# Attention with beacon keys and a two-layer block: where the second layer's last groups stand among the next chunk's first layer

## The chip, the cores and the metric

One core of a Trainium2 chip runs the kernel. The metric is device time in microseconds: 332.71 us, the median of three runs (331.96 to 333.87). A profiled execution took 332.48 us.

## The reference

Attention over 8 sequences (B) with 8 heads (H), 576 tokens (S) and head size 64 (D). Each head's keys and values are preceded by 16 beacon keys and values, which every token may see; the rest is causal. Its output is the input of a two-layer block over 4608 tokens.

```python
k_all = np.concatenate([beacon_k, k], axis=2)
v_all = np.concatenate([beacon_v, v], axis=2)
scores = scale * np.matmul(q, k_all.transpose(0, 1, 3, 2))
causal[:, Nb:] = np.triu(np.ones((S, S), dtype=bool), k=1)
scores = np.where(causal, -1000000000.0, scores)
scores = scores - scores.max(-1, keepdims=True)
a = np.exp(scores)
a /= a.sum(-1, keepdims=True) + 1e-09
attn = np.matmul(a, v_all)
...
x = attn.transpose(0, 2, 1, 3).reshape(B * S, H * D)      # 4608 x 512
h = x @ w_in                                              # 512 x 2048
g = np.maximum(0.01 * h, h)
out = g @ w_out                                           # 2048 x 512
```

## The kernel before

**Attention.** Two heads make a pair; a sequence has four pairs, so there are 32 (g = 0 to 31). The scores stand transposed, keys on the partitions, for five chunks of keys. From pair 8 on the scores of all pairs are one long row of columns (1664 a pair), cut into tiles of 512 columns for both heads; `block(m)` does three tiles: its matmuls (L314), its exps on ScalarE (L329 for the first tile, one head each; L333 for the other two, both heads at once), and then on POOL the causal triangles (L289). The first tile's two heads lie in two PSUM buffers of the pool `ps_one`, the other two tiles in the pool `ps_sc`. `value(g, half)` multiplies probabilities with values (L359: 12 matmuls in half 0, 18 in half 1), and VectorE divides by the sums (L388, L389). `x_turn(g)` lets SP transpose the result by DMA into `xT` (L417, L425), where the first layer reads it.

**The two layers** work on nine chunks of 512 tokens. The first layer has 16 up groups a chunk (`up`, `moe1`): four matmuls of 512 columns into an `acc` of `ps_one` (L442; eight shorter ones in chunk 4), then a PReLU on ScalarE into `gT` (L450). The second layer has down groups (`down`, `moe2`). Chunk 0 has 16 plain ones (L512). The other chunks have 14, eight matmuls of 256 columns each (L539): seven products of a Strassen scheme, two token tiles each, in the order 1, 6, 2, 7, 5, 4, 3. Sums of parts of `gT` that the products need are made on VectorE (L616, `token_sums`), four operations after the eighth and four after the sixteenth up group; `due` hands out one of them at each group, and the third down group of a chunk takes all that are left. Product 1 reads PReLUs, product 6 is the first to read sums.

**PSUM.** `ps_one` has four buffers of one bank each. A tile holds a buffer from its first write to its last read. The second layer's accumulators are "a" (products 1 and 2, down groups 0 to 5), "b" (product 6, groups 2 and 3), "c" (products 7 and 4, groups 6 to 11) and "d" (products 5 and 3, groups 8 to 13).

**The order** is written out by hand up to pair 7. From there a list of events (L792 to L814) places blocks, value halves, loads, transposes and `finish` on a time line counted in pairs, sorted by time; every engine keeps the order in which the program was written. Between events the loop (L817 to L829) lets `fill()` put up and down groups, as many as the share of the time line asks for. A window ends with each sequence; `KEPT = 3` groups are left over at its end, and `finish` sets `held` to 3, so that `fill()` gives these first. Otherwise `fill()` gives an up group if one is possible, and turns are changed where both kinds are possible. Up groups of chunk i need down groups of chunk i - 2 to be done, and down groups of chunk i need all its up groups. Before a value half (L826) at least four groups must stand behind the last block, but only where no down group is left.

So the order of TensorE is fixed when the program is built. Around the first layer of chunk 3 it is (u3.0 is the first up group of chunk 3, d2.8 the ninth down group of chunk 2, V16.1 the second value half of pair 16, B11 block 11):

```
d2.4 B10 d2.5 d2.6 d2.7 d2.8 d2.9 V16.0 d2.10 d2.11 B11 V16.1 d2.12 d2.13
u3.0 u3.1 u3.2 V17.0 u3.3 u3.4 B12 u3.5 u3.6 u3.7 u3.8 V17.1 u3.9 u3.10 V18.0 u3.11 B13
u3.12 u3.13 u3.14 u3.15 V18.1 d3.0 V19.0 d3.1 d3.2 B14 V19.1 d3.3 d3.4
```

After the last value half, of pair 31, the order is d6.3 to d6.13, u7.0 to u7.15, then down groups of chunk 7 and up groups of chunk 8 by turns, then chunk 8's down groups.

Of the kernel before, what the change touches and what calls it, by code (L numbers as in the profile page):

```python
# [15 lines left out]
def kernel(  # L16
# [21 lines left out]
    NF = DF // 128  # L38
# [361 lines left out]
    def x_transposes(g, copy):  # L400
        b, hp = divmod(g, NPAIR)
        x_nat, _ = xs.pop(g)
        ps = ps_one.tile([128, 1024], BF16, name="tp", tag="one")
        for t, (q0, rows) in enumerate(QT):
            nc.tensor.transpose(
                ps[:, q0 : q0 + rows],
                x_nat[0:rows, t].rearrange("p e d -> p (e d)"),
                ident[0:rows, 0:rows],
            )
        copy(out=xT[:, hp, x_at(b) : x_at(b) + S], in_=ps[:, 0:S])  # L410
# [93 lines left out]
    def ND(i):  # L504
        return NF if i == 0 else 2 * len(PRODUCTS)
# [89 lines left out]

    done1, done2, at2, ready, turn, first_down, held = [0], [0], [0, 0], [0], [0], [0], [0]

    def fill():
        i1, fc = divmod(done1[0], NF)
        i2, n2 = at2  # L600
        can1 = i1 < ready[0] and (i1 < 2 or i2 > i1 - 2)
        can2 = i2 < NCH and i2 < i1 and done1[0] >= first_down[0]
        if held[0] and can2:
            held[0] -= 1
            down()
        elif can1 and (turn[0] == 0 or not can2):
            up()
        elif can2:
            down()
        return can1 or can2  # L610
# [14 lines left out]
    def up():  # L625
        i1, n = divmod(done1[0], NF)
        assert i1 < ready[0]
        fc = n if i1 == 0 else n // 2 + n % 2 * HF
        moe1(i1, fc)
        add_due()  # L630
        done1[0] += 1
        turn[0] = 1
        if i1 and n % (2 * SLICE) == 2 * SLICE - 1:
            due.extend((i1, op) for op in token_sums(i1, n // 2 + 1 - SLICE, n // 2 + 1))

    def down():
        add_due()
        if at2[1] == 2:
            add_all(at2[0])
        moe2(*at2)  # L640
        done2[0] += 1
        at2[1] += 1
        if at2[1] == ND(at2[0]):
            at2[:] = at2[0] + 1, 0
        turn[0] = 0
# [19 lines left out]
            )  # L665

    NG = B * NPAIR
    KEPT = 3

    def has(g):  # L670
        return 0 <= g < NG
# [3 lines left out]
    def chunks_with(g):  # L675
        return (g + 1) // NPAIR * S // 512

    def finish(g, eng=0):
        if eng < 2 and g in xs:
            x_transposes(g, (dve, act)[eng])  # L680
        ready[0] = chunks_with(g)
        if g % NPAIR == NPAIR - 1:
            turn[0] = 1
            held[0] = KEPT

    def run(steps):
        for step in steps.split():
# [7 lines left out]
            elif op == "e":  # L695
                value_ahead(*a)
            elif op == "x":
                finish(*a)
            elif op == "l":
                load_qk(*a)  # L700
# [39 lines left out]
    with order:  # L740
# [43 lines left out]
            for parts in tiles:  # L784
                triangles(parts)

        def has_down():
            return at2[0] < done1[0] // NF

        since = 0  # L790
        events = []
        for g in range(FIRST, NG):  # L792
# [14 lines left out]
        for g in range(FIRST, NG):  # L807
            events.append((g + 3.5, 2, finish, (g, 2)))
            if g % NPAIR == NPAIR - 1:
                ends.append(g + 3.5)  # L810
# [6 lines left out]
        for at, _, what, args in events:  # L817
            while w + 2 < len(ends) and at > ends[w + 1]:
                w, d0 = w + 1, done1[0] + done2[0]
            todo = NF * ready[0] + sum(ND(i) for i in range(ready[0])) - KEPT - d0  # L820
            aim = d0 + todo * (at - ends[w]) / (ends[w + 1] - ends[w])
            while done1[0] + done2[0] < aim and fill():
                pass
            if what is block:
                since = done1[0] + done2[0]
            elif what is value and not has_down():  # L826
                while done1[0] + done2[0] < since + 4 and fill():
                    pass
            what(*args)  # L829
        while at2[0] < NCH:  # L830
            fill()
# [30 lines left out]
```

## Time and profile before

| what | value |
|---|---|
| median of 3 runs | 332.71 us |
| profiled execution, its time | 332.48 us |
| its span, first to last instruction | 330.8 us |
| up groups' matmuls (L442) | 134.0 us busy |
| down groups' matmuls (L539) | 111.0 us busy in four rows (47.2, 32.9, 15.5, 15.4) |
| value matmuls (L359) | 39.5 us busy |
| PReLU (L450) | 83.0 us busy, 620 ns each |
| exps of the blocks (L329, L333) | 28.9 and 51.7 us busy |
| granted TensorE clock | 0.999 |

PE is TensorE, PEld its weight loads, DVE VectorE, ACT ScalarE, POOL GpSimd, SP SyncE. In the table of waits, each line has the waiting engine and line, what released it, the total in us, how often, and the longest. A wait that stands at PEld and at PE is one wait seen twice: the weight load waits first, and the matmul behind it. In the timeline a line has start and length in us, the engine, the line, the operation, and in brackets the idle time before it and what ended it. A PE row's first matmul can start some 0.2 us after its weights began to load.

### The profile page before, as it was taken

To read this page: it belongs to the slowest core of one execution; us is meant where nothing else is said; L and a number is where in the kernel's file an instruction comes from. 1 tells how busy PE (TensorE), PEld (TensorE's weight loads), DVE (VectorE), ACT (ScalarE), POOL (GpSimd) and SP (SyncE) were. 2 spreads that over 40 slices of the span, in tenths; PEclk is the share of its full clock that TensorE was granted. 3 is DMA by queue.
4 is the path that set the end of the run, shared out by engine and by line. 5 is a ranking of instruction groups with operands and counts; after the bars stand their busy time and mean duration, and the time that the engine had idled before them with its cause. 6 is when DMAs were issued, how large, how long until landed. Compare 5 with 4: busy or idle time off the path is not lost.

```text
span 330.8 us, 8482 instructions
## 1 busy us (share of the span) xinstructions
PE 317.8 (96%) x3401; PEld 213.1 (64%) x3429; DVE 132.5 (40%) x280; ACT 199.8 (60%) x336; POOL 183.2 (55%) x354
## 2 busy tenths in 40 slices
PE   8999999999899999999999999998999999999996
PEld 5574555455586557844778888655875695466685
DVE  3572357126443145414621453334442642333343
ACT  4969861678665784578645865587458514644420
POOL 8895968979987884669546976686221000000000
PEclk9999999999999999999999999999999999999999
DMA  8999999999999999999989999999431113000113
GB/s 134 140 204 178 153 209 121 179 181 131 180 111 169 158 157 142 131 164 102 145 122 154 109 146 113 184 120 155 55 100 37 36 21 127 2 0 34 64 43 117
DMA packets 155929, 39.93 MB, mean 121 GB/s; under 512 B 143041, under 2 KB 153153, under 8 KB 155889
## 3 DMA queue, kind: packets, MB, share of 16 engines
q0 software_dynamic: 99824, 18.54, 83.1%
q1 hardware_dynamic: 55792, 20.77, 38.7%
q8 instruction: 27, 0.44, 0.6%
q14 instruction: 14, 0.11, 0.1%
q10 hardware_dynamic: 272, 0.07, 0.1%
HBM read 37.22 MB, written 9.44 MB: 141 GB/s over the span
## 4 chain that ended last, share of the span: by engine, by line
PE 76%; DMA 8%; ACT 5%; DVE 4%; POOL 4%; issue 2%; SPq 0%; ACTq 0%; POOLq 0%
PE acc L442 34%; PE acc L539 25%; PE av L359 7%; PE sc L314 5%; DMA w_out_sb<-in_moe_w_out_dram 4%; PE acc L512 4%; DMA v_aug<-in_v_dram 3%; DVE gsum L616 2%; ACT aT L333 2%; ACT aT L329 2%; ACT gT L450 1%; DVE x_nat L389 1%; POOL gsum L158 1%; DMA xT<-x_nat 1%; POOL v_aug L214 1%
## 5 line engine op out<-in xcount | busy, mean ns | idle before, releaser
L442 PE MATMUL acc<-xT,w_in_sb 128*128 128x512 bf16 (+1 forms) x615 | 134.0, 357 | 1.9 <-DMA xT<-x_nat 0.5
L450 ACT ACTIVATE gT<-acc 128x512 bf16<-128x512 f32 x144 | 83.0, 620 | 56.9 <-PE acc L442 55.4
L442 PEld LDWEIGHTS <-w_in_sb 128*128 128x128 bf16 x640 | 59.6, 98 | 53.6 <-issue 4.3
L289 POOL TENSOR_SCALAR_AFFINE_SELECT aT<-aT 128x256 bf16<-128x256 bf16 (+2 forms) x160 | 59.8, 403 | 60.9 <-ACT aT L329 38.7
L539 PEld LDWEIGHTS <-gT 128*128 128x128 bf16 x512 | 48.9, 98 | 11.2 <-ACT gT L450 2.3
L333 ACT ACTIVATE aT<-sc 128x1024 bf16<-128x1024 f32 (+3 forms) x64 | 51.7, 890 | 0.0
L539 PE MATMUL acc<-w_out_sb,gT 128*128 128x256 bf16 x384 | 47.2, 273 | 1.4 <-ACT gT L450 1.3
L329 ACT ACTIVATE aT<-sc 128x512 bf16<-128x512 f32 (+3 forms) x64 | 28.9, 520 | 25.3 <-PE sc L314 25.3
L359 PEld LDWEIGHTS <-aT 128*128 128x128 bf16 (+1 forms) x960 | 36.6, 98 | 9.3 <-issue 3.0
L539 PEld LDWEIGHTS <-gsum 128*128 128x128 bf16 x384 | 36.1, 98 | 8.8 <-DVE gsum L616 3.3
L359 PE MATMUL av<-v_aug,aT 128*128 128x65 bf16 (+1 forms) x960 | 39.5, 194 | 1.9 <-ACT aT L329 1.6
L214 POOL DMA_DIRECT2D v_aug<-in_v_dram x40 | 34.3, 866 | 4.3 <-DMA w_in_sb<-in_moe_w_in_dram 4.0
L171 POOL DMA_DIRECT2D q_nat<-in_q_dram x48 | 34.9, 734 | 0.7
L171 POOL DMA_DIRECT2D k_nat<-in_k_dram x48 | 34.8, 732 | 0.7 <-DMA w_out_sb<-in_moe_w_out_dram 0.4
L539 PE MATMUL acc<-w_sum,gsum 128*128 128x256 bf16 x256 | 32.9, 273 | 1.8 <-DVE gsum L616 1.7
L616 DVE TENSOR_TENSOR gsum<-gT 128x1024 bf16<-128x1024 bf16 x16 | 11.2, 697 | 53.9 <-ACT gT L450 53.9
L389 DVE TENSOR_TENSOR x_nat<-av,rec 128x384 bf16<-128x384 f32 (+1 forms) x64 | 31.4, 490 | 2.2
L388 DVE RECIPROCAL rec<-av 128x6 f32<-128x6 f32 (+1 forms) x64 | 11.9, 185 | 50.7 <-PE av L359 50.5
L276 ACT ACTIVATE aT<-sc 128x1024 bf16<-128x1024 f32 (+3 forms) x32 | 26.0, 874 | 3.7 <-PE sc L267 1.9
L314 PE MATMUL sc<-qT,kT 64*128 64x80 bf16 (+22 forms) x384 | 22.4, 250 | 1.2 <-PE acc L442 0.5
L314 PEld LDWEIGHTS <-kT 64*128 64x128 bf16 x384 | 13.3, 94 | 11.9 <-issue 8.9
L573 DVE TENSOR_TENSOR u<-acc,u 128x512 f32<-128x512 f32 x8 | 5.5, 691 | 27.2 <-PE acc L539 27.2
(63 smaller groups left out, 221.5 us busy)
## 6 DMA issues: line engine op xcount, KB each, us to landing
out_dram<-osb SPq DMA_DIRECT2D x27, 256.0 KB, 2.8
q_nat<-in_q_dram POOLq DMA_DIRECT2D x48, 72.0 KB, 4.8
k_nat<-in_k_dram POOLq DMA_DIRECT2D x48, 72.0 KB, 5.2
v_aug<-in_v_dram POOLq DMA_DIRECT2D x24, 128.0 KB, 6.4
w_in_sb<-in_moe_w_in_dram POOLq DMA_DIRECT2D x2, 1024.0 KB, 12.3
w_out_sb<-in_moe_w_out_dram POOLq DMA_DIRECT2D x2, 1024.0 KB, 11.6
out_dram<-u SPq DMA_DIRECT2D x7, 256.0 KB, 2.3
gsum<-in_q_dram POOLq DMA_DIRECT2D x8, 144.0 KB, 6.4
```

The costliest lines, as they stand in the source:

```text
L171: nc.gpsimd.dma_start(out=t[:, :, par], in_=(q, k)[which][b, 2 * hp + par].rearrange("(t p) d -> p t d", p=NR),)
L214: nc.gpsimd.dma_start(out=dst[lo : ROWS[c], c, :, 0:D], in_=v[b, :, OFF[c] : OFF[c] + n].rearrange("h p d -> p h d"),)
L276: nc.scalar.activation(out=aT[:, :, c0 : c0 + w], in_=sc[:, :, 0:w], func=AF.Exp, scale=0.125)
L289: nc.gpsimd.affine_select(out=view, in_=view, compare_op=ALU.is_ge, fill=0.0, base=128 - n if lo == 0 else 0, channel_multiplier=-1, patte ...
L314: nc.tensor.matmul(out=(sc[par] if apart else sc[:, par])[:, at : at + b - a], lhsT=kT[ps_, c * 128 : (c + 1) * 128], rhs=qT[ps_, q0 : q0 ...
L329: nc.scalar.activation(out=probs[g][:, par, lo:hi], in_=sc[par][:, at : at + hi - lo], func=AF.Exp, scale=0.125)
L333: nc.scalar.activation(out=probs[g][:, :, lo:hi], in_=sc[:, :, at : at + hi - lo], func=AF.Exp, scale=0.125)
L359: nc.tensor.matmul(out=avv[:, n, 0 : D + 1], lhsT=aT[0 : ROWS[c], par, a0 : a0 + 128], rhs=va[0 : ROWS[c], c, 2 * hp + par, :], start=(c = ...
L389: nc.vector.tensor_tensor(out=x_nat[:, t0:t1].rearrange("p t e d -> p (t e) d"), in0=avv[:, :, 0:D], in1=rec[:, n0:n1, None].to_broadcast( ...
L442: nc.tensor.matmul(out=acc[:, lo:hi], lhsT=w_in_cols(fc, j), rhs=xT[:, j, x0 : x0 + hi - lo], start=(j == 0), stop=(j == NJ - 1), skip_gro ...
L450: nc.scalar.activation(out=gT[i][:, fc, :], in_=acc, func=AF.Prelu, alpha=0.01)
L539: nc.tensor.matmul(out=acc[:, lo : lo + HD], lhsT=left(i, n, fc, tile), rhs=right(n, fc), start=(opens and lo == 0 and fc == 0), stop=(fc ...
```

## The change

`KEPT` becomes 6, so that six groups are left over at a sequence's end; a new `LEAD = 3` of them are what `finish` asks `fill()` to give first. The others are kept by a new condition in `fill()`: when the last `LAST = 3` down groups of a chunk are all that is left of it, and the up groups in hand are those of the next chunk, up groups go first. And the rule of four groups between a block and a value half now holds always; `has_down` goes.

```diff
@@ fill
+    LAST = 3
+
     def fill():
         i1, fc = divmod(done1[0], NF)
         i2, n2 = at2
...
-        elif can1 and (turn[0] == 0 or not can2):
+        elif can1 and (turn[0] == 0 or not can2 or (i1 == i2 + 1 and ND(i2) - n2 <= LAST)):
             up()
@@
-    KEPT = 3
+    KEPT, LEAD = 6, 3
@@ finish
-            held[0] = KEPT
+            held[0] = LEAD
@@ the loop over events
-        def has_down():
-            return at2[0] < done1[0] // NF
-
...
-            elif what is value and not has_down():
+            elif what is value:
                 while done1[0] + done2[0] < since + 4 and fill():
                     pass
```

No instruction is added or removed; those of TensorE, ScalarE, VectorE and SP change places, POOL's keep theirs. Around chunk 3 the order becomes:

```
d2.1 B10 d2.2 d2.3 d2.4 d2.5 d2.6 V16.0 d2.7 d2.8 B11 d2.9 d2.10
u3.0 u3.1 V16.1 u3.2 V17.0 u3.3 u3.4 B12 u3.5 u3.6 u3.7 u3.8 V17.1 u3.9 u3.10 V18.0 u3.11 B13
u3.12 u3.13 u3.14 u3.15 V18.1 d2.11 V19.0 d2.12 d2.13 B14 d3.0 d3.1 d3.2 d3.3 V19.1 d3.4
```

At the other chunks, the down groups that now stand behind the next chunk's up groups are:

| up groups of chunk | down groups behind them | between the last up group and the chunk's first down group, before | after |
|---|---|---|---|
| 1 | d0.13 to d0.15 | nothing | d0.13 to d0.15, V10.0, V10.1 |
| 2 | d1.13 | nothing | d1.13, V15.0 |
| 3 | d2.11 to d2.13 | V18.1 | V18.1, V19.0, d2.11 to d2.13, B14 |
| 4 | none | B18 | nothing |
| 5 | d4.12, d4.13 | nothing | d4.12, d4.13, V27.0 |
| 6 | d5.11 to d5.13 | nothing | d5.11 to d5.13, V31.0, V31.1 |
| 7 | d6.11 to d6.13 | nothing | d6.11 to d6.13, then turns |

Around block 5 the order is "B4 u1.14 u1.15 d1.0 d1.1 V10.0 V10.1 d1.2 B5 V11.0" before and "B4 u1.15 d0.13 d0.14 d0.15 V10.0 V10.1 d1.0 B5" after.

## Prediction

> **What bounds the kernel now.** I read the engine rows first, then TensorE's waits, then the timelines of ScalarE and VectorE around a score block. The profiled execution took 332.48 us with a span of 330.8; the median of the three runs is 332.71, so the two agree, and every sum below is made against 332.48.
>
> ```profile
> span 330.8 us, 8482 instructions
> PE 317.8 (96%) x3401; PEld 213.1 (64%) x3429; DVE 132.5 (40%) x280; ACT 199.8 (60%) x336; POOL 183.2 (55%) x354
> PE 76%; DMA 8%; ACT 5%; DVE 4%; POOL 4%; issue 2%; SPq 0%; ACTq 0%; POOLq 0%
> ...
> PEld L539 <- DVE gsum L616: 3.3, 6, 0.8
> PEld L539 <- ACT gT L450: 2.3, 3, 0.9
> PE av L359 <- ACT aT L329: 1.6, 3, 0.8
> PE acc L442 <- DMA xT<-x_nat: 0.5, 1, 0.5
> PE sc L314 <- DMA kT<-k_nat: 0.4, 1, 0.4
> PE sc L314 <- DVE x_nat L389: 0.3, 1, 0.3
> ```
>
> TensorE is busy 96% of the span, and the number of its instructions doesn't change. So the change can only move the time through TensorE's waits (columns: total us, times, longest). The first two are the second layer starting on a chunk whose first layer has just ended: a chunk's first down group waits for the last PReLUs, its third for the token sums on VectorE. The third is a value half that follows a score block at once and needs a PSUM buffer that the block's exps still hold.
>
> **What it removes.** With three (or one or two) down groups of the old chunk standing between the new chunk's last up group and its first down group, the 2.3 and the 3.3 us go; with four groups between a block and the next value half, the 1.6 go; block 5 then no longer follows values of pair 10 closely, 0.3. Sum 7.5 us at most. The 0.9 us behind DMAs I leave as they are. Between the last value half (pair 31) and chunk 7's first up group stand 11 down groups before and after, so that transpose stays hidden.
>
> **What it adds: PSUM buffers held.** The pool `ps_one` has four buffers, which up groups (`acc`), value halves (`av`) and each block's two `sc1` tiles share with the second layer. Of a chunk's 14 down groups, product 7 opens accumulator "c" at d6, last written by product 4 at d11; product 5 opens "d" at d8, last written by product 3 at d13. Before, both are closed when the next chunk's up groups begin. After, keeping d11 to d13 back holds two of the four through the up groups of chunks 3, 6 and 7, and keeping d13 (or d12, d13) holds one through those of chunks 2 and 5; in chunk 1, d13 to d15 of the plain layer hold one. Chunk 4 holds none: the three led groups were the last three. Counting buffers along the new order, as the built program places them, the next user of a buffer now comes two groups after the last one 77 times (4 before), three groups after 77 times (64 before), and at once 6 times (3 before).
>
> What that costs is read from a block in the middle of up groups: first ScalarE, then TensorE, at block 8, then two up groups of chunk 7 without blocks.
>
> ```profile
> 112.70 0.60 ACT L450 ACTIVATE gT<-acc 128x512 bf16<-128x512 f32 x1 [0.82 <-PE acc L442]
> 113.20 1.08 ACT L329 ACTIVATE aT<-sc 128x512 bf16<-128x512 f32 x2
> 114.15 1.96 ACT L333 ACTIVATE aT<-sc 128x1024 bf16<-128x1024 f32 x2
> 115.96 2.11 ACT L450 ACTIVATE gT<-acc 128x512 bf16<-128x512 f32 x4
> ...
> 112.60 0.83 PE L314 MATMUL sc<-qT,kT 64*128 64x400 bf16 x12
> 113.36 3.63 PE L442 MATMUL acc<-xT,w_in_sb 128*128 128x512 bf16 x16
> ...
> 277.16 0.60 ACT L450 ACTIVATE gT<-acc 128x512 bf16<-128x512 f32 x1 [0.27 <-PE acc L442]
> 278.02 0.60 ACT L450 ACTIVATE gT<-acc 128x512 bf16<-128x512 f32 x1 [0.27 <-PE acc L442]
> ```
>
> A block occupies TensorE 0.8 us but ScalarE until 116.1, 3.5 us after its start. The PReLU of the first up group behind it starts only at 115.96 and gives its buffer back at about 116.6; TensorE has by then run four up groups (0.87 us each, from the 0.86 between PReLUs at 277.16 and 278.02). With four buffers that just fits, and no wait stands there now.
>
> - *One buffer held:* the fourth up group behind the block needs the first one's buffer. It is ready at 113.36 + 3 x 0.87 = 115.97 and waits until 116.65: 0.67 us. That holds for blocks 2, 3, 8, 20 and 21 (behind blocks 4, 9 and 22 kept down groups stand in that place, behind block 7 the 0.5 us for the transposed activations covers it): 5 x 0.67 = 3.3 us.
> - *Two held:* the third up group waits for the first one's PReLU: 116.65 - 115.1 = 1.55 us. And one of the block's `sc1` tiles takes the buffer of the up group just before it, whose PReLU ends 0.7 us after the block's start (112.60 to 113.30): blocks 12 and 25, whose first tile is cut into two key chunks, start all their exps 0.7 us later, 2.25 each; block 13, whose first half tile is whole, hides most of that, 1.7. Sum 6.2 us.
> - *Two held, between blocks:* an up group's buffer is free when its PReLU ends. In chunk 7 ScalarE rests 0.27 us between PReLUs, so two buffers just suffice: 16 groups at 0 to 0.1, I take 0.02 each, 0.3. Where a value half (0.55 us of TensorE) stands in place of an up group (0.87), the PReLU misses by about 0.25, or VectorE's reciprocal and multiply (0.20 and 0.56) by 0.1: some five such places in each of chunks 3 and 6, 0.85 and 1.0. Sum 2.1.
>
> **What it moves.** Chunk 4's first down group now follows its last two up groups, which follow block 18: the pattern of the old 0.9 us waits (u14, u15, d0 behind block 22); by the PReLU's 4.0 us behind the block against 3.4, 0.65. The third down groups of chunks 2 and 5 now need a buffer that value halves' multiplies free, behind the sums: 0.3 and 0.5. Worst is block 5. The plain layer's d13 to d15 come after u15, so VectorE gets in a row three sums (0.6 each once they run back to back), the copy of the output, and the weight difference:
>
> ```profile
> 75.27 0.69 DVE L521 COPY osb<-acc 128x512 f32<-128x512 f32 x1 [1.09 <-PE acc L512]
> 75.88 1.21 DVE L465 TENSOR_TENSOR w_out_sb<-w_out_sb 128x2048 bf16<-128x2048 bf16 x1
> ```
>
> and behind them pair 10's reciprocals and multiplies, whose buffer block 5 takes. The sums start 4.05 us after block 4 (u15's PReLU), the difference ends at 4.05 + 3 x 0.63 + 0.6 + 1.2 = 7.7, pair 10's first reciprocal and multiply at 8.5. Between the blocks TensorE has one up group, three plain down groups, both value halves and d0: 0.8 + 0.7 + 3 x 0.87 + 1.0 + 1.1 = 6.2. Block 5 waits 2.3 us. Together 3.75 us.
>
> SP's stores of d11 and d13 go out later, behind the transposes of the next pairs; an issue takes about 0.5 us of SP and nothing waits for a store within a chunk. POOL's queue keeps its order. The probabilities' four buffers have a pair to spare. I cost these at nothing; the cover is the slack between a pair's transpose landing and its use (pair 15's second was issued at 131.5 us and takes the 4.9 of the DMA table, chunk 3 begins at 140.4: 4 us), and without it the 0.5 us wait would repeat at each of six chunks, 3 us.
>
> **Sum.** -7.5 + 3.3 + 6.2 + 2.1 + 3.75 = +7.85: 332.48 + 7.85 = 340.3 us. Bounds: the gain 6 to 8.4 (the DMA waits gone too); one buffer 0 (exps overtaken) to 5 x 0.9; two buffers 2.1 (only the 0.7 stays) to 8; between blocks 0 to 5; moved 1.5 to 5. All low ends at once make -4.8, all high ends +16.5, 327.7 and 349; they won't come together, so I go half the way from the sum to each: 334 to 344.5.
>
> [...] The row is the 3.5 us of exps that four up groups just cover. [...]
>
> [...] The row is the granted clock, 9 tenths or more in every slice though waits of 0.9 us stand among them. [...] I go by the row.
>
> **Rivals.**
> 1. *The buffers held cost nothing, faster.* The place is the third and fourth up group behind a block; the price would be zero if PReLUs ran ahead of the exps. For it: ScalarE is busy only 60%, and chunk 7's PReLUs keep up. Against: ScalarE works in order and the four PReLUs start at 115.96, behind the exps. Only the moved waits then stay: 332.48 - 7.5 + 3.75 = 328.7. It decides if the waits on held buffers add up to under 2.3 us (7.5 - 3.75, less the 1.5 that can be told). Chance 0.13.
> 2. *Both sides cancel:* a third of the 11.6 us on held buffers comes, since one wait covers the next: -7.5 + 3.9 + 3.75 = +0.1, 332.6. For it: block 7's wait is such a one. Against: the blocks stand 7 to 8 us apart. Chance 0.07.
> 3. *Every up group with two buffers pays,* not only those behind blocks: 48 groups x 0.2 more, 350; or the clock falls. Against: the 0.27 us of rest. Chance 0.05.
> 4. *The change doesn't do what it says.* The order is fixed when the program is built, and the kept groups do stand there; only in chunk 4 none are kept. That is in the sum.
>
> **How the numbers follow.** The forecast, slower by the held buffers, has 0.75, rival 3 the remaining 0.05. About 0.5% (1.7 us) is what a measurement of this kernel can tell: faster, under 331.0, 0.13 from rival 1; within, 0.07 from rival 2; slower 0.75 + 0.05 = 0.80. The forecast's own range is 334 to 344.5; to hold 8 in 10 it reaches a little toward rival 2, to 333.5, and leaves out rivals 1 and 3.
>
> **What would show it.** TensorE's waits of a down group on PReLU and sums fall from 5.6 us to under 2; the value halves' 1.6 go. In their place come waits of up groups (L442) on PReLU of 0.6 us and more behind blocks 2, 3, 8, 20, 21, of over 1 us behind 12, 13 and 25, of score matmuls on a PReLU at 12 and 25, and 2 us of block 5 on the multiply of pair 10. Wrong if up groups show no waits on PReLU, or if the clock falls below 9 tenths.

## The result, and the profile after

The changed kernel took 344.57 us, the median of four runs (344.08 to 344.92), against 333.27 for the kernel before, run beside it (331.96 to 333.87): a ratio of 1.0343 [1.0306, 1.0381]. It is slower by 11.3 us. The prediction was 340.3 us with a range of 333.5 to 344.5, so the direction was right and the time lies just above the range. The profiled execution took 344.42 us with a span of 342.7, which is 11.9 us more than before on both counts. The ratios, here and below, leave out runs more than 1.5% longer than the fastest of the same kernel; the medians do not.

First the page's head of the changed kernel, and the shares of its chain of waits:

```profile
span 342.7 us, 8475 instructions
PE 322.2 (94%) x3401; PEld 215.7 (63%) x3429; DVE 131.3 (38%) x280; ACT 200.4 (58%) x336; POOL 183.5 (54%) x354
PE 75%; ACT 16%; DVE 3%; DMA 3%; issue 2%; ACTq 0%; SPq 0%; DVEq 0%
```

TensorE does the same 3401 matmuls, and its share falls from 96 to 94%. In the chain that ended last, ScalarE's share goes from 5 to 16%. VectorE's share falls from 4 to 3% and the DMAs' from 8 to 3%, and GpSimd's 4% is gone. Most of the time went into waits on ScalarE. TensorE's own table of waits, and one line of its weight loads', name them (total us, times, longest):

```profile
PE acc L442 <- ACT gT L450: 6.9, 13, 0.9
PE sc L314 <- DVE x_nat L389: 1.7, 1, 1.7
PE sc L314 <- DMA kT<-k_nat: 1.4, 2, 0.9
PE sc L314 <- ACT gT L450: 1.2, 3, 0.4
...
PE sc L314 <- DVE osb L521: 0.7, 1, 0.7
...
PEld L539 <- ACT gT L450: 0.9, 1, 0.9
```

Of the 5.6 us that down groups' weight loads waited for PReLUs and sums, 0.9 is left, once (the last line; 0.7 at the matmul behind it). The value halves' 1.6 us are gone. In their place up groups wait 13 times for a PReLU, 6.9 us in all, where before there was no such line. Score blocks (sc) wait on the four things shown. A wait in this table is an idle stretch only, and TensorE also loses a little at starting again (at block 8 below, 0.69 us for a wait of 0.53). So below I count a place by its *step*: from the first weight load of a group to the first weight load of the next, less what the same step takes where nothing waits (0.86 us an up group, 0.87 a down group, 0.78 a block).

**One buffer held.** TensorE, then ScalarE, at block 8 of the changed kernel:

```profile
115.58 0.83 PE L314 MATMUL sc<-qT,kT 64*128 64x400 bf16 x12
116.34 2.77 PE L442 MATMUL acc<-xT,w_in_sb 128*128 128x512 bf16 x11
119.64 1.02 PE L442 MATMUL acc<-xT,w_in_sb 128*128 128x512 bf16 x4 [0.53 <-ACT gT L450]
```

```profile
116.18 1.08 ACT L329 ACTIVATE aT<-sc 128x512 bf16<-128x512 f32 x2
117.13 1.96 ACT L333 ACTIVATE aT<-sc 128x1024 bf16<-128x1024 f32 x2
118.94 2.35 ACT L450 ACTIVATE gT<-acc 128x512 bf16<-128x512 f32 x4
```

Three up groups run behind the block, and the fourth waits. Its buffer is that of the first, whose PReLU starts only at 118.94, behind the exps, and ends near 119.5. The step is 0.69 us too long. Such a step stands behind blocks 2, 3, 7, 8, 20 and 21: 0.71, 0.76, 0.64, 0.69, 0.57 and 0.69, together 4.06 us.

**Two buffers held.** TensorE at block 12:

```profile
147.59 0.36 PE L314 MATMUL sc<-qT,kT 64*128 64x448 bf16 x1
148.34 0.81 PE L314 MATMUL sc<-qT,kT 64*128 64x448 bf16 x13 [0.39 <-ACT gT L450]
149.44 1.89 PE L442 MATMUL acc<-xT,w_in_sb 128*128 128x512 bf16 x7 [0.28 <-ACT aT L329]
152.25 1.89 PE L442 MATMUL acc<-xT,w_in_sb 128*128 128x512 bf16 x8 [0.93 <-ACT gT L450]
```

Three waits follow one another: the block's second tile for the PReLU of the up group ahead of it, the first up group for the first tile's exp, and the third up group for the first one's PReLU. Blocks 12, 13 and 25 cost 2.09, 1.62 and 2.09 us, together 5.80.

**Two buffers held, away from the blocks' exps.** TensorE in chunk 3, where value halves (L359) stand among up groups:

```profile
144.93 0.54 PE L359 MATMUL av<-v_aug,aT 128*128 128x65 bf16 x12
145.77 1.89 PE L442 MATMUL acc<-xT,w_in_sb 128*128 128x512 bf16 x8 [0.31 <-ACT gT L450]
```

A value half lasts 0.54 us, too short for the PReLU of the up group ahead of it (0.60 us, from 145.12), so the up group behind it waits 0.31. Such places cost 1.54 us in chunk 3 and 1.71 in chunk 6. In chunk 7, which has neither blocks nor value halves, the windows (span, busy us of PE, PEld, DVE, ACT and POOL, granted clock, then the DMAs' share and GB/s) show none:

```profile
286.00:300.00 14.00, 13.95 (x71) 7.01 (x72) 3.26 (x6) 9.30 (x16) 0.00 (x0) 1.00 0.05 19
```

TensorE is busy 13.95 of 14.00 us on two buffers, at a clock of 1.00.

**Block 5.** TensorE and VectorE of the changed kernel, and a window there:

```profile
88.94 1.04 PE L539 MATMUL acc<-w_out_sb,gT 128*128 128x256 bf16 x8
90.67 0.17 PE L314 MATMUL sc<-qT,kT 64*128 64x16 bf16 x1 [0.69 <-DVE osb L521]
92.51 1.47 PE L314 MATMUL sc<-qT,kT 64*128 64x16 bf16 x15 [1.67 <-DVE x_nat L389]
93.91 1.78 PE L539 MATMUL acc<-w_out_sb,gT 128*128 128x256 bf16 x8
```

```profile
87.78 0.83 DVE L618 TENSOR_TENSOR gsum<-gT 128x1024 bf16<-128x1024 bf16 x1 [4.04 <-ACT gT L450]
...
89.94 0.68 DVE L521 COPY osb<-acc 128x512 f32<-128x512 f32 x1
90.54 1.21 DVE L465 TENSOR_TENSOR w_out_sb<-w_out_sb 128x2048 bf16<-128x2048 bf16 x1
...
91.89 0.56 DVE L389 TENSOR_TENSOR x_nat<-av,rec 128x384 bf16<-128x384 f32 x1
```

```profile
92.00:95.40 3.40, 2.89 (x23) 1.81 (x24) 1.56 (x4) 2.18 (x5) 2.16 (x5) 0.50 1.95 194
```

VectorE runs the sums, the copy, the weight difference and only then pair 10's division, as predicted. Block 5 waits 0.69 + 1.67 = 2.36 us. Then, for 3.4 us, the granted clock is 0.50 (in the next 2.6 us it is 0.99): the 15 matmuls take 1.47 us instead of some 0.8, and the next down group 1.78 instead of 1.04. The block's step is 3.23 us too long and that of d1.1 0.75, where the waits alone are 2.36. Of the 1.6 us between, some 0.3 go into starting again (in the experiment below that issues the difference later, the same place is 1.47 us too long for waits of 1.2 at a whole clock). About 1.4 are the clock's.

**The keys.** TensorE at blocks 1 and 2:

```profile
63.56 0.78 PE L314 MATMUL sc<-qT,kT 64*128 64x384 bf16 x12 [0.50 <-DMA kT<-k_nat]
69.91 0.72 PE L314 MATMUL sc<-qT,kT 64*128 64x256 bf16 x10 [0.92 <-DMA kT<-k_nat]
```

Before, these two blocks ran without a wait, at 64.37 and 69.56. Now they come at 62.82 and 68.69, because keeping six groups instead of three at the first window's end leaves fewer groups to put ahead of them. SP issued the transposes of their keys at 57.4 and 60.8 us in both kernels. TensorE has come earlier and the transposes have not. The two steps are 0.67 and 1.09 us too long. That is one execution: in those of two experiments below with the same order here, block 1 did not wait and block 2 lost 1.1 us (the difference later) and 2.2 (the difference three times).

### The profile page after: what moved, and what is told of

Read it like the earlier page. It is cut to its first block, busy times and chain, and to the rows that moved or that the text cites. A ratio compares the mean times of both kernels' runs of the same rounds, so it can differ in the third digit from the quotient of the medians.

```text
span 342.7 us, 8475 instructions
## 1 busy us (share of the span) xinstructions
PE 322.2 (94%) x3401; PEld 215.7 (63%) x3429; DVE 131.3 (38%) x280; ACT 200.4 (58%) x336; POOL 183.5 (54%) x354
## 4 chain that ended last, share of the span: by engine, by line
PE 75%; ACT 16%; DVE 3%; DMA 3%; issue 2%; ACTq 0%; SPq 0%; DVEq 0%
PE acc L442 27%; PE acc L539 26%; ACT aT L333 8%; PE av L359 7%; PE sc L314 5%; ACT gT L450 5%; ACT aT L329 3%; DMA kT<-k_nat 3%; PE sc L267 2%; PE acc L512 2%; PE av L653 2%; PE tp L243 1%; DVE x_nat L389 1%; DVE gsum L618 1%; ACT aT L276 1%
## 5 line engine op out<-in xcount | busy, mean ns | idle before, releaser
L442 PE MATMUL acc<-xT,w_in_sb 128*128 128x512 bf16 (+1 forms) x615 | 135.5, 357 | 9.1 <-ACT gT L450 6.9
L289 POOL TENSOR_SCALAR_AFFINE_SELECT aT<-aT 128x256 bf16<-128x256 bf16 (+2 forms) x160 | 58.9, 396 | 70.9 <-ACT aT L329 41.4
L359 PEld LDWEIGHTS <-aT 128*128 128x128 bf16 (+1 forms) x960 | 36.1, 98 | 8.0 <-issue 1.5
L539 PEld LDWEIGHTS <-gsum 128*128 128x128 bf16 x384 | 36.9, 98 | 6.7 <-DVE x_nat L389 1.0
L359 PE MATMUL av<-v_aug,aT 128*128 128x65 bf16 (+1 forms) x960 | 38.7, 194 | 0.3
L539 PE MATMUL acc<-w_sum,gsum 128*128 128x256 bf16 x256 | 31.4, 273 | 0.6 <-DVE x_nat L389 0.6
L314 PE MATMUL sc<-qT,kT 64*128 64x80 bf16 (+21 forms) x384 | 24.6, 255 | 5.3 <-DVE x_nat L389 1.7
L314 PEld LDWEIGHTS <-kT 64*128 64x128 bf16 x384 | 14.4, 95 | 16.9 <-issue 10.3
L539 PE MATMUL acc<-w_sum,gT 128*128 128x256 bf16 x128 | 16.3, 272 | 0.0
```

Source lines behind the costliest of these rows:

```text
L289: nc.gpsimd.affine_select(out=view, in_=view, compare_op=ALU.is_ge, fill=0.0, base=128 - n if lo == 0 else 0, channel_multiplier=-1, patte ...
L314: nc.tensor.matmul(out=(sc[par] if apart else sc[:, par])[:, at : at + b - a], lhsT=kT[ps_, c * 128 : (c + 1) * 128], rhs=qT[ps_, q0 : q0 ...
L359: nc.tensor.matmul(out=avv[:, n, 0 : D + 1], lhsT=aT[0 : ROWS[c], par, a0 : a0 + 128], rhs=va[0 : ROWS[c], c, 2 * hp + par, :], start=(c = ...
L442: nc.tensor.matmul(out=acc[:, lo:hi], lhsT=w_in_cols(fc, j), rhs=xT[:, j, x0 : x0 + hi - lo], start=(j == 0), stop=(j == NJ - 1), skip_gro ...
L539: nc.tensor.matmul(out=acc[:, lo : lo + HD], lhsT=left(i, n, fc, tile), rhs=right(n, fc), start=(opens and lo == 0 and fc == 0), stop=(fc ...
```

## The experiments

The first chunk's part of the program, some 58 us, varies between runs of one kernel by a few us. So beside the timed ratio I give, from each profiled execution, the stretch from chunk 1's first up group to the end: 272.5 us before, 284.9 after.

**The value rule alone**, on the order before.

```diff
-            elif what is value and not has_down():
+            elif what is value:
```

> The kernel before with one part of the change alone: the rule of four groups between a block and the next value half holds always; three groups are left at a sequence's end and none is kept behind the next chunk's up groups. Theory (held PSUM buffers cost the time): no buffer is held, so up groups wait for PReLUs less than 1 us in all; the 1.6 us of value halves behind blocks go, while the third down groups of chunks 2 and 5 come closer to the last up groups (+1.2, +0.6): 331 to 333.5, like before. Rival (the rule itself costs, since it pulls groups ahead of values): 336 or more.

Measured: 333.41 us against 333.18, ratio 0.9995 [0.9963, 1.0027], stretch 270.7. The value halves' line is gone from the waits, and the matmuls' wait on sums is 3.5 us where it was 1.7 before:

```profile
PE acc L539 <- DVE gsum L616: 3.5, 4, 1.6
```

The rule gives no time that can be told, and up groups still don't wait for PReLUs. So the loss is not the value rule's.

**The kept groups alone**, on the order after.

```diff
-            elif what is value:
+            elif what is value and not at2[0] < done1[0] // NF:
```

> The changed kernel with its other part alone: groups are kept behind the next chunk's up groups, but a value half follows a block at once where a down group is left, which is now nearly always. Theory (held buffers): 23 times instead of 6 the next user of a buffer comes directly behind the last one, mostly a value half behind a block's exps at 0.5 to 0.8 us each: 12 us or more above the changed kernel's lower bound, 348 or more. Rival (the rule for values is what costs): 338 or less.

Measured: 358.25 us, ratio 1.0732 [1.0664, 1.0801], stretch 295.4. The leading lines of its waits:

```profile
PE acc L442 <- ACT gT L450: 9.0, 15, 1.2
PE sc L314 <- ACT gT L450: 4.7, 10, 0.6
```

The keeping of groups brings the loss, and the value rule softens it: value halves that follow a block closely take buffers that the exps hold. Up groups wait for exps 10 times here, 2.8 us in all, against 2 times and 0.6 us in the changed kernel. In this order a buffer is given to the next user at once at 23 places, against 6 in the changed kernel. The two parts don't add: the same rule is worth nothing on one order and 13.7 us (358.25 - 344.57) on the other.

**Two buffers held, nothing moved.** On the order before, two tiles of `ps_one` that no one reads are kept open from the third to the last up group of chunks 3 and 6. Each is touched by one small matmul at the start and one at the end.

```diff
+    HELD, dummies = (3, 6), []
+    def touch():
+        for t in dummies:
+            nc.tensor.matmul(out=t[:, 0:16], lhsT=blank, rhs=blank[:, 0:16], start=True, stop=True)
...
+        if i1 in HELD and n == 2:
+            dummies[:] = [ps_one.tile([128, 512], FP32, name="dummy", tag="one") for _ in range(2)]
+        if i1 in HELD and n == 2:
+            touch()
...
+        if i1 in HELD and n == NF - 1:
+            touch()
```

> The kernel before, its order untouched, but through chunks 3 and 6 (from the third up group to the last) two buffers of the pool ps_one are held by tiles that nothing uses (two matmuls of 16 columns each at either end, 0.3 us in all). Theory (held buffers): blocks 12, 13 and 25 cost 2.1, 1.6 and 2.1 us, the places between them 3.2: before + 9, 341 to 342.5. Rival (the order of the groups costs, not the buffers): before + 0.3, 333.

Measured: 342.41 us, ratio 1.0235 [1.0183, 1.0287], stretch 281.1, so 8.5 more than before. Its block 12, the timeline of TensorE:

```profile
146.95 0.36 PE L314 MATMUL sc<-qT,kT 64*128 64x448 bf16 x1
147.70 0.81 PE L314 MATMUL sc<-qT,kT 64*128 64x448 bf16 x13 [0.39 <-ACT gT L450]
148.80 1.67 PE L442 MATMUL acc<-xT,w_in_sb 128*128 128x512 bf16 x7 [0.28 <-ACT aT L329]
151.61 1.67 PE L442 MATMUL acc<-xT,w_in_sb 128*128 128x512 bf16 x7 [1.14 <-ACT gT L450]
```

The waits of the changed kernel return one by one without its order: 0.39, 0.28 and then about 1 us, 2.09 in the steps of blocks 12 and 25, 1.62 in block 13's. This shows the mechanism directly.

**One buffer held, nothing moved**: the same with one tile, in chunks 2 and 5 (one run, no interval).

> The kernel before, its order untouched, with one buffer of ps_one held by an unused tile from the third up group to the last in chunks 2 and 5. Theory (one held buffer makes the fourth up group behind a block wait for the first one's PReLU): 0.6 to 0.7 us behind blocks 8 and 21, up to as much behind 7 and 20, nothing else: before + 1.3 to 2.7 from the first up group of chunk 1 to the end. Rival (three buffers suffice, the waits in the changed kernel come from its order): before + 0.2.

Measured: 336.89 us, stretch 275.7, so 3.2 more than before. A longer wait at the start of chunk 1, where nothing is held, makes 1.2 of it. The wait that was sought is this line:

```profile
PE acc L442 <- ACT gT L450: 2.0, 4, 0.5
```

It stands behind blocks 7, 8, 20 and 21, with steps 0.61, 0.69, 0.61 and 0.69 too long, 2.6 us in all. Block 7's was not covered here either.

**Two groups kept back instead of three**, on the order after.

```diff
-    LAST = 3
+    LAST = 2
```

> The changed kernel with two down groups kept instead of three: product 4 then closes accumulator c before or early in the next chunk's up groups, and only one buffer is held through chunks 3, 6 and 7, as through 2 and 5. Theory (the price goes by how many buffers are held): blocks 12, 13 and 25 fall from 2.1, 1.6 and 2.1 us to 0.7 each, the 3.2 us between them nearly vanish: 6 to 7 us below the changed kernel, 337.5 to 339. Rival (any held buffer costs the same, or the kept groups' place costs): 343 or more.

Measured: 336.39 us, ratio 1.0093 [1.0055, 1.0131], stretch 274.9. With d11 done in time, accumulator "c" is closed, and only "d" is held.

```profile
PE acc L442 <- ACT gT L450: 4.0, 8, 0.6
PE sc L314 <- DVE x_nat L389: 1.7, 1, 1.7
```

No wait of an up group is above 0.6 us now. Blocks 12 and 25 cost 0.68 each and block 13 0.59, in place of 2.09, 2.09 and 1.62, and the waits between blocks go too. It came out better than expected: its profiled execution had no waits for keys at blocks 1 and 2, and block 5 lost 2.3 us instead of 4.0. Block 5's second wait is as long as before, 1.67 us, but here the clock stayed whole (0.999 in the profiled execution).

**The weight difference later**, on the order after: out of the way of pair 10's division.

```diff
-            if n2 == NF - 1:
-                weight_sums(1)
...
+        if (i, n2) == (1, 4):
+            weight_sums(1)
```

> The changed kernel; the weight difference on VectorE (1.2 us) is issued at chunk 1's fifth down group instead of behind the plain layer's last one. Theory (the queue on VectorE ahead of pair 10's multiply makes block 5 wait, and that wait of 2.4 us lets the TensorE clock halve for 3.4 us): the wait shrinks by 1.2 us, the clock stays whole, another 1.4 us go: 341.7 to 342.3. Rival (the clock falls because of all the short waits since 60 us): the half-clock stretch stays, only 1.2 us go, 343.4.

Measured: 343.42 us, ratio 1.0265 [1.0222, 1.0307]. The times alone don't decide between the two expectations. Its profiled execution took 6.4 us more ahead of chunk 1, so I take its stretch from there: 282.0, 2.8 less than after. Its second wait at block 5, and the window there:

```profile
PE sc L314 <- DVE x_nat L389: 0.5, 1, 0.5
```

```profile
90.00:100.00 10.00, 8.72 (x93) 5.90 (x93) 4.59 (x9) 5.86 (x10) 9.45 (x18) 1.00 2.08 170
```

The wait falls from 1.67 to 0.53 us, about the 1.2 of the difference, and the clock is whole there and in all six runs of this kernel. The block's step is 1.47 us too long in place of 3.23 + 0.75. Of the 2.5 us that the place lost less, 1.1 are the wait, and about 1.4 the half clock that went with it.

**The difference three times**, on the order after, to see the clock again.

```diff
-            tt(out=b12, in0=b22, in1=b12, op=SUB)
+            [tt(out=b12, in0=b22, in1=b12, op=SUB) for _ in range(3)]
```

Subtracting three times gives the same as once, but for rounding: b22 - (b22 - (b22 - b12)).

> The changed kernel with the weight difference on VectorE made three times instead of once (b22 - (b22 - (b22 - b12)), the same but for rounding). Theory (block 5 waits behind VectorE, and a wait of some 2.5 us or more halves the clock): block 5's wait grows from 2.5 to 4.9 us, the clock is halved in every run around 92 to 97 us: 346.5 to 348.5. Rival (VectorE's queue isn't what block 5 waits for): 344.5, unchanged.

Measured: 352.1 us (two runs, 350.63 and 353.57), ratio 1.0572 [1.0486, 1.0657]. TensorE and a window at block 5:

```profile
97.36 1.47 PE L314 MATMUL sc<-qT,kT 64*128 64x16 bf16 x15 [4.19 <-DVE x_nat L389]
```

```profile
96.00:100.00 4.00, 2.63 (x21) 1.63 (x22) 2.38 (x6) 1.92 (x5) 0.71 (x2) 0.53 0.84 74
```

The wait grew from 1.67 to 4.19 us, by two differences of 1.2, and the clock was halved twice as long: 6.83 us, against 3.41 in the changed kernel. A second halving of 3.41 us came with a wait of 2.0 us on keys at block 2. The total missed the expectation by 3.6 us; part of it is this second halving, the rest is open.

**Three groups left over in the first window, six later**, on the order after: meant to take away the waits on keys and block 5's.

```diff
-            todo = NF * ready[0] + sum(ND(i) for i in range(ready[0])) - KEPT - d0
+            todo = NF * ready[0] + sum(ND(i) for i in range(ready[0])) - (KEPT if w else LEAD) - d0
```

> The changed kernel with three groups instead of six left over in the first stretch (sequence 2) alone, so that three more groups go ahead of blocks 1 to 5; the later windows as changed. Theory: blocks 1 and 2 no longer come before the transposed keys that SP issued at the same time in both kernels (0.5 and 0.9 us), block 5 stands behind four more groups and its wait of 2.5 us and the half clock go, chunk 1's last down group isn't kept into chunk 2 (two waits of 0.65 us less), chunk 2's first down group comes right behind its last up groups (+0.4): 338 to 340. Rival (the first stretch only has the misfortune of one profile): 343 or more.

Measured: 343.02 us, ratio 1.034 [1.0258, 1.0421], stretch 282.3, above the 338 to 340 expected. Both waits went, and the clock stayed whole (1.0), but another wait came:

```profile
PE acc L442 <- DMA xT<-x_nat: 2.7, 1, 2.7
```

Chunk 2's first up group now waits 2.7 us for the transposed activations. The last of the transposes ahead of it were issued at 102.4 us, and TensorE is there at 104.1. In the changed kernel they were issued at 101.3 and TensorE came at 108.7: the time lost on the way had covered them.

**Another cure for the old waits, nothing held**, on the order before: when a block is due and a chunk has at most four up groups left, they go ahead of the block, so that their PReLUs come before its exps.

```diff
+                while done1[0] % NF >= NF - 4 and done1[0] // NF < ready[0]:
+                    up()
```

> The kernel before; where four or fewer up groups of a chunk are left when a block is due, these go first, so that their PReLUs run ahead of the block's exps; no buffer is held and the rule for values is as before. Theory (the 5.6 us before a chunk's first and third down group come from PReLUs queued behind exps): most of them go, the values' 1.6 us stay: 328 to 329.5. Rival (other waits take their place): 331 or more.

Measured: 329.75 us, ratio 0.9899 [0.9852, 0.9946], a little above the range expected. The profiled execution is the slowest of the five (332.23 us), with a stretch of 272.1, hardly less than before, so the gain stands on the times alone. The wait of down groups on PReLUs is gone. Those on sums (1.7 us before, at the matmuls), which the expectation had mostly gone, and the value halves' stay, and two blocks now wait for keys:

```profile
PE acc L539 <- DVE gsum L616: 2.0, 6, 1.1
PE sc L314 <- DMA kT<-k_nat: 2.0, 2, 1.5
PE av L359 <- ACT aT L329: 1.7, 3, 0.8
```

**This and the value rule together.** The edit is that of the last experiment and that of the first.

> The kernel before with the last up groups of a chunk ahead of a block that is due, and with the change's rule of four groups between a block and the next value half; nothing kept, no buffer held. Theory: it takes out what the change was to take out (2.3 + 3.3 + 1.6 us) and adds no wait of up groups: 325.5 to 328, faster than both kernels. Rival (transposes by DMA come late for the blocks that stand earlier): 330 or more.

Measured: 329.74 us, ratio 0.9897 [0.9857, 0.9937], stretch 268.0. It beats both kernels, and is no better in time than the last one alone. It was expected at 325.5 to 328 us. What is missing stands in these waits of its profile:

```profile
PE sc L314 <- DVE x_nat L389: 1.3, 3, 0.5
PE acc L442 <- DMA xT<-x_nat: 1.1, 1, 1.1
...
PE acc L539 <- DVE gsum L616: 0.2, 1, 0.2
```

The down groups' and value halves' waits on PReLUs, sums and exps, 1.3, 1.7 and 1.6 us at the matmuls before, are down to 0.2 without one more buffer held. Part of them came back as the wait for activations, 1.1 us, and as blocks waiting for value halves' divisions, 1.3.

## Why the prediction was right, and where it was wrong

The terms of the prediction's sum, and what the profile of the changed kernel has at the same places:

| term | predicted us | measured us | how |
|---|---|---|---|
| waits that go | -7.5 | about -8.4 | the stretch's +12.3 less the losses below |
| one buffer held | +3.3 | +4.1 | six steps |
| two held, at blocks 12, 13, 25 | +6.2 | +5.8 | three steps |
| two held, between blocks | +2.1 | +3.3 | chunks 3 and 6; chunk 7 nothing |
| moved | +3.75 | +5.9 | d4.0 0.72, d2.2 0.47, d5.2 0.70, block 5 with d1.1 3.98 |
| keys' transposes | 0 | +1.8 | blocks 1 and 2 |

The first term is what remains after the others, so it carries their errors. By name, the waits that went make 7.2 us: 5.6 - 0.9 of down groups, 1.6 of value halves, 0.5 for activations, 0.4 of block 9 for keys. The 0.3 at block 5 that the prediction counted did not go: that wait grew to 1.67. Measured against the prediction's own bounds, one term lies outside, "moved" (5.9 against 1.5 to 5), and the keys had no bound.

**Right.** The mechanism and its places: buffers held over the next chunk's up groups, priced from ScalarE's 3.5 us behind a block. The experiment that only holds two buffers shows the same waits at blocks 12, 13 and 25, and keeping two groups instead of three takes them away. At those blocks the working was right to 0.4 us in 6.2, and the wait of block 5 to 0.1 (2.3 against 2.36). Rival 1 (held buffers cost nothing) and rival 2 (both sides cancel) fell. Rival 3's main claim, that every up group on two buffers pays 0.2 us, fell in chunk 7: two buffers sufficed there without a wait, and TensorE was busy 13.95 of 14.00 us.

**Wrong: the clock at block 5.** The failed step is "Block 5 waits 2.3 us", taken as the whole price, and with it "I go by the row". The row was the clock of 9 tenths or more beside waits of up to 0.9 us. It said nothing of a wait of 2.4 us, which the same prediction worked out. With such a wait the clock halved for 3.41 us, which cost about 1.4 us more in the profiled execution. The experiment that moves the difference shows it: the wait is shorter by 1.1, the place by 2.5. Without this 1.4 the profiled execution would have taken 343.0, inside the range. The prediction's own sign of being wrong, a clock below 9 tenths, came in one of the page's 40 slices:

```profile
PEclk9999999999899999999999999999999999999999
```

The price in timed runs is less certain and may be smaller: of the changed kernel's four runs the one with a clock of 0.998 was only 0.6 us shorter than the mean of the other three, at 0.994 to 0.995. The clause of rival 3, "or the clock falls", thus came about in one place, by two waits close together and not by many short ones.

**Wrong: a cost of nothing for SP and the DMAs.** The prediction named the cover, "the slack between a pair's transpose landing and its use", from pair 15 alone and for activations alone. The keys' transposes of blocks 1 and 2 had less slack. They were issued as before and were needed 1.5 and 0.9 us earlier: 1.8 us in this execution (1.1 and 2.2 in two others).

**Sized too small.** "Behind block 7 the 0.5 us for the transposed activations covers it": that wait was not there in the changed kernel, nor with one buffer held on the order before, and the held buffer's 0.64 us stood there itself. Between blocks the term of 2.1 was 3.3: the part for chunk 7 (0.3) was nothing, and chunks 3 and 6 cost nearly double their 0.85 and 1.0. The third down groups of chunks 2 and 5 lost 0.47 and 0.70 in place of 0.3 and 0.5.

**Which waits halve the clock.** Not the length of one wait decides. The wait of 1.67 us at block 5 stands in the kernel that keeps two groups as well, and one of 2.7 us on activations where three groups are left over in the first window; the clock stayed whole in both places (0.999 and 1.0 over their profiled executions). But the halvings lie whole steps of 3.41 us apart: in the changed kernel they begin at 92.03 and, at its very end, at 344.62, 74 steps apart, and the first is 25 steps behind the start of the clock's record at 6.70. Before, the one halving begins at 329.91, 95 steps behind the start of the record at 5.64. So count TensorE's idle time in one such step. The changed kernel's step ahead of the halving, and the two steps around block 5 in the kernel that keeps two groups:

```profile
88.62:92.03 3.41, 1.52 (x25) 1.09 (x21) 3.35 (x6) 0.00 (x0) 3.41 (x6) 1.00 1.73 155
...
87.39:90.81 3.42, 2.18 (x40) 1.70 (x38) 3.09 (x5) 0.27 (x1) 3.42 (x6) 1.00 2.33 149
90.81:94.22 3.41, 2.62 (x32) 2.16 (x33) 2.42 (x7) 2.11 (x5) 2.37 (x6) 1.00 1.74 197
```

In the first, both waits fall into one step: 3.41 - 1.52 = 1.89 us idle. In the other kernel the idle time is split over two steps: 1.24 and 0.79 us, and no halving. A step near the end of the changed kernel, then one of the kernel before and the rest behind it:

```profile
337.78:341.20 3.42, 1.76 (x17) 1.33 (x14) 1.54 (x3) 0.00 (x0) 0.00 (x0) 1.00 0.55 185
...
326.49:329.90 3.41, 1.12 (x11) 0.76 (x8) 0.95 (x3) 0.00 (x0) 0.00 (x0) 1.00 0.46 154
329.91:330.77 0.86, 0.00 (x0) 0.00 (x0) 0.00 (x0) 0.00 (x0) 0.00 (x0) 0.50 0.00 0
```

With 1.66 us idle the clock stayed whole in the step behind, with 2.29 it was halved. The step ahead of 344.62 was idle throughout, 3.41 us. In these two profiles, from the start of the clock's record on, every halving stands behind a step with 1.89 us idle or more, and no step with 1.66 or less has one behind it. That is three halvings in all: it tells what happened here and sets no limit for other runs. The steps begin differently in the two executions (6.70 and 5.64), so whether block 5 pays is partly luck: judged by their mean clocks (0.994 to 0.995, against 0.998), three of the changed kernel's four runs did.

## What to carry to other kernels

Before work is moved past other work, count what it leaves open: here accumulators in a shared pool of four buffers, worth 0.6 to 0.8 us at each block with one held and 1.6 to 2.1 with two, more than the waits that the move removed. Price a held buffer at the place where the engine that empties the pool is furthest behind, and look for an order that feeds that engine earlier instead: up to four up groups ahead of the block gave 1%. When TensorE comes earlier, list what else was only just in time, transfers above all, and don't take a clock read beside short waits for the clock beside long ones that fall close together.

## What the runs showed of the hardware that was not expected

The clock was halved for 3.41 us behind a step of 3.41 us with 1.89 us of idle time in two waits (0.69 and 1.67), and for 6.83 us where the same two waits were 0.70 and 4.19. Where the idle time was split over two steps (1.24 and 0.79 us), with a wait of the same 1.67 us, it stayed whole, and so it did with a wait of 2.7 us (1.0 in that profiled execution). Two buffers for 16 up groups in a row cost TensorE nothing in chunk 7 (busy 13.95 of 14.00 us), at a clock of 1.00, and the 13 waits of up groups for PReLUs (0.9 us at most) left the clock whole too: it is 1.00 from 6.70 to 92.03 and from 95.45 to the last instruction.
